# A fused attention and two-MLP kernel: the whole program emitted from one list of operations, with written places for its buffers

## The chip, the cores and the metric

The kernel runs on one core of a Trainium2 chip. TensorE (PE in the profile) multiplies matrices into PSUM, VectorE (DVE), ScalarE (ACT) and GpSimd (POOL) do elementwise work, and SyncE (SP) issues the DMAs. Each engine takes its instructions strictly in the order in which the program emits them. The metric is the time of one execution in device microseconds. Lower is better.

## The reference

```python
q_s = softmax(q over the head dimension); k_s = softmax(k over the sequence)   # float32
kv  = einsum('bhsd,bhse->bhde', k_s, v)
x   = einsum('bhsd,bhde->bhse', q_s, kv)      # 4 batches x 576 tokens -> (2304, 512)
xn  = x / sqrt(mean(x*x) + 1e-6) * rms_g
g   = xn @ w_gate;  val = xn @ w_val          # 512 x 1536, float64 weights
x2  = (silu(g) * val) @ w_out                 # 1536 x 512
out = softplus(x2 @ w2_in) @ w2_out           # 512 x 2048, 2048 x 512
```

Weights arrive in float64 and are converted on the chip. Every product of the MLPs is made from operands split into a high and a low half (`mm3`): three matmuls for each.

## The kernel before, in words

The 2,304 tokens are six blocks `j` of 384. The work has four stages.

1. **Attention and the first third of layer a, from a list.** `ORDER` is a text of 793 entries that a loop emits one by one (L907). It holds the attention, the first 24 weight fetches and conversions, and the first 16 steps of the gate and value products (4 of the 12 slices of `w_gate`, taken plainly) with 15 output steps. Each entry is an operation and its arguments, the last letter being the engine: V for VectorE, P for GpSimd, A for ScalarE. `B.n` emits n filler matmuls of `ident` into a bank that nobody reads (L782).
2. **The rest of those steps** (8 of 24), in a Python loop.
3. **Layer a, Strassen-like.** The other 8 slices are taken in pairs: 12 units (four weight pairs by three pairs of token blocks). A unit has seven products (`SEVEN`) for the gate and seven for the value, each six matmuls of 384 columns (`seven`, L1150), whose sums are copied or added out of PSUM (L1277, L1280), go through silu (L1282, L1288), the product (L1284, L1291) and a split into halves (L1259, L1260). Then come eight output groups of six matmuls (`acc`), which start from a copy of the running sum into PSUM (L1189) and end with a copy back (L1199).
4. **Layer b.** 24 units of seven products `h` (six matmuls each; L1385, L1388, softplus L1322, halves L1324, L1326) and 12 groups of three matmuls of 512 columns (`yacc`, L729 to L731).

Beside these, `convert_some` takes up weight conversions as "jobs" when an estimate of spent engine time (`credit`) allows: absolute value (L253, L249), clamp (L258), three bit operations (L264, L268, L272), sums of pairs (L329 to L332), high half (L310) and low half (L315). Converted weights of layer b and of `w2_out` are written to DRAM from three tiles `ws` (L318, kept<-ws) and read back as `wb` for each unit (L1219). Split token blocks ("quads", L1016 to L1033) go out and come in in the same way (L1037, L1040, L1009, L1012). `advance`, `need`, `more` and `background` decide in the emitting code where these fall between the products; tiles come from rings that turn in the order of use (`w` 16 places, `ws` 3, `raw` 2, `hl` 6, `hb` 5), and PSUM banks are tied to a use (two for each of gate and value, four for `acc`, and so on). All DMAs are issued by SP in one queue, in the order of emission.

In the attention, the values are summed over five chunks of the keys' sequence: four of 128 rows and one of 64 (`k3`, L569).

Of the kernel before, what the change touches and what calls it, by code (L numbers as in the profile page):

```python
# [10 lines left out]
I32 = mybir.dt.int32  # L11
# [14 lines left out]
LQ.0.0 Q0.0.0 QS.0.0.0.V LQ.0.1 LX.0 QE.0.0.0 MX.0 QS.0.0.1.P LK.0.0.1 Q0.0.1 QS.0.1.1.V LK.0.2.2 MK K0.0.0.1.1.R MV  # L26
K0.0.2.2.1.V QE.0.1.1 K0.0.2.2.2.V QE.0.0.1 QS.0.1.0.P LK.0.1.1 K0.0.2.2.3.V LQ.0.2 QE.0.1.0 K0.0.0.1.2.R F.3 LW.0
K0.0.0.1.3.R K0.0.1.1.1.V F.6 K0.0.2.2.4.V F.10 K0.0.1.1.2.V K0.0.0.1.4.R QR.0.0 QI.0.0 QR.0.1 K0.0.1.1.3.V B.29
K1.0.2 KM.0.2 QM.0.0.1.P QI.0.1 CA.3 K0.0.1.1.4.V Q0.0.2 B.9 K1.0.0 K2.0.2 QM.0.1.0.P QS.0.2.0.P CA.10 T.1 CA.6 KM.0.0
K2.0.0 CL.3.V KS.0.2 KS.0.0 QM.0.1.1.P LV.0.4.8 QE.0.2.0 CL.6.V CD.3.0 CD.6.0 CL.10.V QM.0.0.0.P LV.0.0.4 T.2 KE.0.2  # L30
MX.1 CD.3.1 QR.0.2.0 TC.2.A B.4 T.0 CD.10.0 KE.0.0 TC.0.A LQ.1.0 B.1 K3.0.2 F.0 TC.1.A CD.3.2 CA.0 CD.6.1 K3.0.0
CD.10.1 LX.1 QI.0.2.0 Q0.1.0 K4.0.2 K4.0.0 B.2 X0.0.1 CL.0.V LK.1.0.2 LG X0.0.0 CD.6.2 QM.0.2.0.P X0.0.3 CD.10.2
CD.0.0 XG.0.3.A LK.1.2.2 SQ.0.3 CC.6 X0.0.2 F.5 LQ.1.1 QS.1.0.1.P LW.1 QS.1.0.0.P SQ.0.2 K0.1.0.2.1.V CD.0.1
K0.1.0.2.2.V K0.1.2.2.1.V K0.1.0.2.3.V SQ.0.1 LV.1.0.4 K0.1.2.2.2.V QE.1.0.1 K0.1.0.2.4.V K0.1.2.2.3.V CA.5 F.7 CD.0.2
K0.1.2.2.4.V B.3 K1.1.0 SQ.0.0 B.1 K1.1.2 CC.3 CL.5.V XS.0.0.1.P XG.0.2.A XG.0.0.A KM.1.0 LV.1.4.8 KM.1.2 CD.5.0
K2.1.2 K2.1.0 XS.0.2.3.P Q0.1.1 XS.0.0.2.P T.3 X1.0 QS.1.1.1.P QE.1.0.0 KS.1.0 QR.1.0 QS.1.1.0.P XD.0 QI.1.0 T.4 XP.0
CC.0 KE.1.0 QM.1.0.0.P B.3 X2.0 QE.1.1.1 XG.0.1.A KS.1.2 QE.1.1.0 LK.2.0.2 CC.10 K3.1.0 KE.1.2 TC.3.A QR.1.1 CD.5.1
X3.0.2 X3.0.0 CD.5.2 HH.0.0.A QI.1.1 LK.2.2.2 TC.4.A T.5 LX.2 K4.1.0 K3.1.2 QM.1.0.1.P F.1 CS.10.P QM.1.1.0.P CS.3.V
F.4 TC.5.A X3.0.3 X3.0.1 MX.2 K0.2.2.2.1.V HH.0.2.A K4.1.2 X0.1.1 K0.2.2.2.2.V T.6 F.2 X0.1.0 HH.0.3.A X0.1.3
K0.2.0.2.1.R X0.1.2 XG.1.1.A LQ.2.0 QM.1.1.1.P LV.2.4.8 LW.2 HH.0.1.A SQ.1.0 SQ.1.1 SQ.1.2 K0.2.2.2.3.V K0.2.0.2.2.R  # L40
CS.0.P XG.1.2.A T.7 K0.2.2.2.4.V TC.7.A HL.0.0.P K0.2.0.2.3.R SQ.1.3 G.1.0 XS.1.0.1.V K0.2.0.2.4.R T.8 K1.2.2 HL.0.1.P
TC.8.A XS.1.2.3.P TC.6.A CA.1 KM.2.2 XG.1.0.A XG.1.3.A G.1.1 XS.1.0.2.P HL.0.3.P K1.2.0 CA.4 K2.2.2 X0.2.0 HL.0.2.V
G.1.2 CA.7 KM.2.0 KS.2.2 CL.1.V Q0.2.0 KE.2.2 CD.1.0 X1.1 F.9 CL.4.V X0.2.2 K2.2.0 CC.5 G.1.3 XD.1 X0.2.1 CS.6.P
CD.1.1 XP.1 KS.2.0 K3.2.2 X0.2.3 SQ.2.1 LQ.2.1 CS.5.V S.1 CL.7.V SQ.2.0 QS.2.0.1.P CD.1.2 CD.4.0 LV.2.0.4 CA.2
XG.2.0.A G.0.0 X2.1 CL.2.V G.0.1 CC.1 CA.9 G.0.2 Q0.2.1 MX.3 KE.2.0 CD.7.0 CD.4.1 CD.7.1 QS.2.0.0.V CS.1.P CD.4.2
CD.2.0 CD.7.2 XG.2.1.A CL.9.V QE.2.0.1 V.0 QE.2.0.0 G.0.3 QR.2.0 CC.4 S.0 CD.9.0 LV.3.4.8 K3.2.0 X3.1.0 G.2.0 XG.2.3.A
A.0 G.2.1 CS.4.P CD.9.1 V.1 X3.1.1 X3.1.2 CD.2.1 QI.2.0 CC.7 CD.9.2 F.8 QS.2.1.1.P A.1 CC.9 CS.7.P G.2.2 G.2.3 AH.1.A
X3.1.3 LK.3.0.2 QM.2.0.0.P K4.2.0 CD.2.2 CS.9.P V.2 AL.1.P LK.3.2.2 S.2 AH.0.A CA.8 AL.0.V G.3.0 T.9 HH.1.0.A CC.2 A.2
QM.2.0.1.V G.3.1 QS.2.1.0.P SQ.2.3 F.11 QE.2.1.1 K4.2.2 SQ.2.2 QE.2.1.0 V.3 LX.3 XS.2.0.1.V CS.2.P G.3.2 T.10 HH.1.1.A
# [30 lines left out]
def linear_attention_swiglu_softplus_kernel(  # L80
# [1357 lines left out]
```

## Time and profile before

| | us |
|---|---|
| three runs, median (lowest to highest) | 940.3 (937.82 to 942.64) |
| the profiled execution: span from the first to the last instruction | 941.6 |
| TensorE busy in it | 898.6 |
| VectorE busy | 594.6 |
| ScalarE busy | 494.4 |
| GpSimd busy | 174.0 |

The span of the profiled execution lies 1.3 us above the median of the runs and inside their range; the profile lists no time outside its span. "Busy" of TensorE includes the time in which a matmul drains while the next one streams, so it is no measure of how much work is left to save. The first `g` matmul starts at 53.6 us, the first matmul of a gate product of layer a's units at 240.2, the first `h` at 534.3.

### The profile page before, as it was taken

To read this page: it belongs to the slowest core of one execution; us is meant where nothing else is said; L and a number is where in the kernel's file an instruction comes from. 1 tells how busy PE (TensorE), PEld (TensorE's weight loads), DVE (VectorE), ACT (ScalarE), POOL (GpSimd) and SP (SyncE) were. 2 spreads that over 40 slices of the span, in tenths; PEclk is the share of its full clock that TensorE was granted. 3 is DMA by queue.
4 is the path that set the end of the run, shared out by engine and by line. 5 is a ranking of instruction groups with operands and counts; after the bars stand their busy time and mean duration, and the time that the engine had idled before them with its cause. 6 is when DMAs were issued, how large, how long until landed. Compare 5 with 4: busy or idle time off the path is not lost.

```text
span 941.6 us, 13520 instructions
## 1 busy us (share of the span) xinstructions
PE 898.6 (95%) x4840; PEld 837.2 (89%) x4840; DVE 594.6 (63%) x1043; ACT 494.4 (53%) x1013; POOL 174.0 (18%) x162
## 2 busy tenths in 40 slices
PE   7799999999999799999999799999999999999997
PEld 7689999999999799998898798888989898889896
DVE  7999997766776698887778867572632223222222
ACT  3586543424776677776667673443543334333332
POOL 4566513211121111211111122221000000000000
PEclk9999999999999899999999989999999999999999
DMA  9983533442757689687598629889367565286502
GB/s 233 258 204 102 156 101 115 126 130 74 305 214 298 236 327 333 238 344 279 187 351 315 252 76 395 292 301 380 102 223 279 179 191 177 98 334 196 168 13 67
DMA packets 111523, 203.52 MB, mean 216 GB/s; under 512 B 30305, under 2 KB 71265, under 8 KB 111457
## 3 DMA queue, kind: packets, MB, share of 16 engines
q1 hardware_dynamic: 111456, 202.67, 64.2%
q8 instruction: 38, 0.62, 0.3%
q14 instruction: 29, 0.23, 0.1%
HBM read 155.19 MB, written 47.45 MB: 215 GB/s over the span
## 4 chain that ended last, share of the span: by engine, by line
PE 56%; DVE 20%; DMA 9%; ACT 9%; issue 4%; POOL 1%; SPq 1%; DVEq 0%; ACTq 0%; POOLq 0%
PE yacc L730 5%; PE yacc L731 5%; PE yacc L729 5%; PE h L731 5%; PE h L730 5%; PE h L729 5%; DMA kept<-ws 4%; PE acc L729 3%; PE acc L730 3%; PE acc L731 3%; PE g L729 2%; PE v L729 2%; PE g L731 2%; PE g L730 2%; PE v L730 2%
## 5 line engine op out<-in xcount | busy, mean ns | idle before, releaser
L1388 DVE TENSOR_TENSOR p<-h,p 128x384 f32<-128x384 f32 x72 | 40.0, 555 | 139.2 <-PE h L731 132.6
L729 PE MATMUL h<-quad,wb 128*128 128x384 f32 x336 | 113.6, 338 | 5.0 <-DVE p L1388 3.0
L730 PE MATMUL h<-quad,wb 128*128 128x384 f32 x336 | 114.6, 341 | 0.0
L731 PE MATMUL h<-quad,wb 128*128 128x384 f32 x336 | 114.5, 341 | 0.0
L1322 ACT ACTIVATE p<-p 128x384 f32<-128x384 f32 x72 | 37.9, 527 | 111.5 <-DVE p L1388 111.4
L729 PE MATMUL yacc<-wb,hb 128*128 128x512 f32 x210 | 82.0, 390 | 1.4 <-ACT y L1338 1.4
L731 PE MATMUL yacc<-wb,hb 128*128 128x512 f32 x210 | 82.8, 394 | 0.0
L730 PE MATMUL yacc<-wb,hb 128*128 128x512 f32 x210 | 82.8, 394 | 0.0
L1385 ACT COPY p<-h 128x384 f32<-128x384 f32 x72 | 34.4, 480 | 85.6 <-PE h L731 85.0
L729 PEld LDWEIGHTS h<-quad,wb 128*128 128x128 f32 x336 | 63.4, 189 | 14.2 <-DVE p L1388 4.3
L730 PEld LDWEIGHTS h<-quad,wb 128*128 128x128 f32 x336 | 63.2, 188 | 7.1
L729 PE MATMUL v<-quad,w 128*128 128x384 f32 x168 | 57.8, 344 | 9.0 <-DVE p L1280 7.8
L731 PEld LDWEIGHTS h<-quad,wb 128*128 128x128 f32 x336 | 63.4, 189 | 0.0
L729 PE MATMUL g<-quad,w 128*128 128x384 f32 x168 | 57.4, 342 | 2.6 <-ACT p L1277 2.4
L1260 POOL TENSOR_TENSOR hb<-p,hb 128x384 fp32r<-128x384 f32 x26 | 28.9, 1111 | 161.4 <-ACT hb L1259 131.4
L731 PE MATMUL v<-quad,w 128*128 128x384 f32 x168 | 57.0, 339 | 0.0
L730 PE MATMUL v<-quad,w 128*128 128x384 f32 x168 | 56.9, 339 | 0.0
L731 PE MATMUL g<-quad,w 128*128 128x384 f32 x168 | 56.6, 337 | 0.0
L730 PE MATMUL g<-quad,w 128*128 128x384 f32 x168 | 56.4, 336 | 0.0
L729 PE MATMUL acc<-h,w 128*128 128x384 f32 x152 | 51.8, 341 | 3.8 <-ACT acc L1189 3.8
L272 DVE SCALAR_TENSOR_TENSOR bits<-raw,bits 128x512 int32<-128x512 int32 x62 | 51.4, 831 | 1.6
L730 PE MATMUL acc<-h,w 128*128 128x384 f32 x152 | 51.5, 339 | 0.0
(200 smaller groups left out, 2440.5 us busy)
## 6 DMA issues: line engine op xcount, KB each, us to landing
wb<-kept SPq DMA_DIRECT2D x120, 512.0 KB, 6.0
quad<-outside SPq DMA_DIRECT2D x30, 768.0 KB, 7.6
kept<-ws SPq DMA_DIRECT2D x40, 512.0 KB, 4.8
raw<-in_moe_w_out_dram SPq DMA_DIRECT2D x26, 512.0 KB, 4.0
outside<-quad SPq DMA_DIRECT2D x12, 768.0 KB, 3.7
quad<-outside SPq DMA_DIRECT2D x24, 384.0 KB, 6.5
raw<-in_moe_w_in_dram SPq DMA_DIRECT2D x16, 512.0 KB, 4.2
outside<-quad SPq DMA_DIRECT2D x18, 384.0 KB, 3.1
```

What stands on the lines that cost most here:

```text
L272: nc.vector.scalar_tensor_tensor(out=b, in0=words[:, :, 0], scalar=29, in1=b, op0=ALU.logical_shift_right, op1=ALU.bitwise_or)
L729: nc.tensor.matmul(out=ps, lhsT=wh, rhs=xh, start=first, stop=False, skip_group_check=more)
L730: nc.tensor.matmul(out=ps, lhsT=wh, rhs=xl, start=False, stop=False, skip_group_check=more)
L731: nc.tensor.matmul(out=ps, lhsT=wl, rhs=xh, start=False, stop=last, skip_group_check=more)
L1260: nc.gpsimd.tensor_tensor(out=h[:, 1], in0=a, in1=h[:, 0].bitcast(F32), op=ALU.subtract)
L1322: nc.scalar.activation(out=ln, in_=src, func=AF.Softplus)
L1385: nc.scalar.copy(out=t, in_=bk[b])
L1388: nc.vector.tensor_tensor(out=t, in0=bk[b], in1=t, op=ALU.add)
```

## The change

`ORDER` becomes a text of 3,517 entries that emits the whole program, and a second text, `HOMES`, lists for each kind of buffer (`ps`: the eight PSUM banks; `w`, `raw`, `bits`, `ws`, `h`, `hl` and others) the place that each taking of one gets. `convert_some`, `need`, `advance`, `background`, `more` and the loops over units go. The number of places stays (16 `w`, 3 `ws`, 2 `raw`, 3 `bits`, 6 `hl`, 7 `h`). What is computed, and how, stays too, but for the fifth chunk of the keys: its matmuls take 128 rows, of which the upper 64 of the values are set to zero once.

New operations: `M` gate or value product, `C` copy, `D` sum, `SI` silu, `U` product, `BH`/`BL` halves of an activation, `OP`/`OM`/`OC` output group (copy in, matmuls, copy out), `H`, `HC`, `HD`, `SP` the same for layer b, `Y`, `YE`, `YO` its output, `F`, `CA`, `CL`, `CD` fetch and conversion, `PS` sums of pairs, `WH`/`WL`/`KO` halves of a weight and its store, `WB` load of a stored weight, `ZS`, `ZH`, `ZL`, `ZO`, `ZI` sum, halves, store and load of a quad. The entries ahead of the first `G` are 233, ahead of the first `M` 902, ahead of the first `H` 2,232.

Engines change by entry. Ahead of the first `H`, on VectorE and formerly on ScalarE: 19 `BH`, 27 `WH` (22 of 512 columns), 10 `ZH`, 11 `C`, 17 `OC`, 24 `OP`, 7 `CA`. On VectorE and formerly on GpSimd: 33 `BL`. On GpSimd and formerly on VectorE: 30 `WL` (24 of 512 columns), 28 `PS`, 4 `ZL`, 2 `ZS`. Filler matmuls: `B` of 114 in place of 52 (two instructions each); 110 of them stand ahead of the first `G`. VectorE's entries ahead of the first `G` come to 89 instructions. One more load of ScalarE's table (`PL`) and one more clearing of 64 x 512 elements by GpSimd (in `MV`) are added.

```diff
 ORDER = """
-LQ.0.0 Q0.0.0 QS.0.0.0.V LQ.0.1 LX.0 QE.0.0.0 MX.0 QS.0.0.1.P LK.0.0.1 Q0.0.1 QS.0.1.1.V LK.0.2.2 MK K0.0.0.1.1.R MV
...
+LQ.0.0 Q0.0.0 LQ.0.1 QS.0.0.0.P QS.0.0.1.V Q0.0.1 LK.0.1.1 QE.0.0.1 LX.0 MK QE.0.0.0 K0.0.1.1.1.V B.3.7 K0.0.1.1.2.V
...
+M.5.6.g KO.33.2 OM.4.1.2 OC.4.1.2.A CL.37.V BL.5.0.0.V OM.4.0.0 CD.37.0 CD.36.2 D.6.1.g WH.35.1.V SI.5.5 SI.5.6 U.5.5
+OP.4.0.2.A BL.5.1.1.V M.6.2.g WL.35.1.V M.6.3.g WH.36.1.A ZI.5.22.hl OM.4.0.2 ZI.5.21.qe0 KO.34.1 OM.4.0.1 C.6.0.v.A U.5.6
...
+HOMES = """
+ps 01234567012346071326405614265014263751463046727544710251327432574621574301261213741562710625327451366301740610
...
+ws 0120122210012012010201201210120122021021020010212010020102100120120102021022102102
+ln 010110100101010110101001
...
-    def ring(name="w"):
-
-        n = ring_n[0]
-        ring_n[0] += 1
-        assert n < NW or n - NW in ring_free, n
-        w = w_p.tile([P, 2, 512], F32R, tag="w", name=name)
-        return w, n
+    def take(pool, key, shape, dtype=F32):
+
+        key += next(turns[key]) if key in turns else ""
+        at, kind, tile_ = homes.get(key, (pool, None, None))
+        if kind != dtype:
+            tile_ = at.tile(shape, dtype, tag=key, name=key, bufs=1)
+            homes[key] = at, dtype, tile_
+        return tile_
+    def bank():
+        return take(ps_p, "ps", [P, 512])
+    def ring():
+        return take(w_p, "w", [P, 2, 512], F32R)
...
             for r in range(R + 1):
-                p = P if r < R else SX
                 nc.tensor.matmul(
-                    out=ps[:, i, :], lhsT=ke_t[lo][:p, i, r], rhs=v_t[:p, m, r, :], start=(r == 0), stop=(r == R)
+                    out=ps[:, i, :], lhsT=ke_t[lo][:, i, r], rhs=v_t[:, m, r, :], start=(r == 0), stop=(r == R)
                 )
...
         def v_ones(_=None):
             nc.gpsimd.memset(v_t[:, :, :, 2 * D:], 1.0)
+            nc.gpsimd.memset(v_t[SX:, :, R, :2 * D], 0.0)
...
+        def a_copy(u, k, n, e):
+            tag = "ln" if k == 2 else {"g": "s", "v": "a"}[n]
+            t = part[u, k, n] = take(late[0] if k == 2 else fa, tag, [P, T])
+            copy[e](out=t, in_=bk[u, n, SEVEN[k][3]])
+        def load_b(u, name):
+            n = 256 if name == "hx4" else 512
+            w = wb[name, u] = ring()
+            nc.sync.dma_start(out=w[:, :, :n].bitcast(F32), in_=kept[name, u % NPB])
...
-        for t in ORDER.split():
-            t = t.split(".")
-            ops[t[0]](*(int(x) if x.isdigit() else x for x in t[1:]))
-        listed[0] = False
+        for t in ORDER.split():
+            t = t.split(".")
+            ops[t[0]](*(int(x) if x.isdigit() and not (i == 1 and t[0] in texts) else x for i, x in enumerate(t[1:])))
```

## Rows read from the trace of the kernel before

**Rows 1.** The page's first part: busy us (share of the span) and instructions.
```profile
PE 898.6 (95%) x4840; PEld 837.2 (89%) x4840; DVE 594.6 (63%) x1043; ACT 494.4 (53%) x1013; POOL 174.0 (18%) x162
```
**Rows 2.** Busy time by stretch: length, then each engine's busy us (instructions), clock, DMA.
```profile
0.00:53.60 53.60, 42.98 (x275) 37.90 (x276) 46.52 (x99) 26.28 (x46) 30.45 (x36) 0.97 1.08 255
53.60:240.20 186.60, 185.71 (x1099) 178.54 (x1098) 154.23 (x287) 93.80 (x171) 64.11 (x54) 1.00 0.41 116
240.20:534.30 294.10, 278.68 (x1550) 270.21 (x1550) 235.44 (x398) 208.98 (x468) 51.16 (x47) 0.98 0.77 285
534.30:941.60 407.30, 391.27 (x1921) 350.54 (x1919) 158.43 (x262) 165.35 (x331) 28.26 (x26) 0.99 0.60 207
...
186.00:228.00 42.00, 42.00 (x244) 42.00 (x243) 29.32 (x45) 14.53 (x30) 6.54 (x6) 1.00 0.35 115
```
**Rows 3.** Timeline of TensorE in layer b: start us, us.
```profile
849.70 0.39 PE L729 MATMUL yacc<-wb,hb 128*128 128x512 f32 x1
...
850.39 0.33 PE L729 MATMUL h<-quad,wb 128*128 128x384 f32 x1
...
851.46 0.39 PE L729 MATMUL yacc<-wb,hb 128*128 128x512 f32 x1
```
**Rows 4.** Whom TensorE waited for, 240.2 to 534.3: us, times, longest.
```profile
PE v L729 <- DVE p L1280: 7.8, 2, 7.4
PE acc L729 <- ACT acc L1189: 3.1, 3, 1.9
```
**Rows 5.** Timeline around 304 us: start us, us, idle before and its releaser.
```profile
310.27 0.41 ACT L310 CAST ws<-sums 128x256 fp32r<-128x256 f32 x1 [9.50 <-DMA kept<-ws]
...
311.66 0.69 PE L729 MATMUL v<-quad,w 128*128 128x384 f32 x1 [7.39 <-DVE p L1280]
```
**Rows 6.** Chain that ended last: start us, us, what.
```profile
121.06 2.81 PE kvp L569 x20
128.20 0.67 PE rsb L701 x6
```
**Rows 7.** VectorE by line, 240.2 to 534.3: busy, mean ns, idle before.
```profile
L272 DVE SCALAR_TENSOR_TENSOR bits<-raw,bits 128x512 int32<-128x512 int32 x34 | 31.0, 911 | 1.2
L268 DVE SCALAR_TENSOR_TENSOR bits<-raw,bits 128x512 int32<-128x512 int32 x34 | 27.1, 798 | 0.3
L1280 DVE TENSOR_TENSOR p<-g,p 128x384 f32<-128x384 f32 x36 | 19.9, 552 | 1.0 <-PE g L731 0.5 <-ACT p L1277 0.3
L1284 DVE TENSOR_TENSOR p<-p,p 128x384 f32<-128x384 f32 x35 | 19.6, 559 | 4.1 <-ACT p L1282 0.5
L264 DVE TENSOR_SCALAR bits<-bits 128x512 int32<-128x512 int32 x34 | 19.4, 572 | 1.2
...
L315 DVE TENSOR_TENSOR ws<-bits,ws 128x512 fp32r<-128x512 f32 x21 | 14.4, 688 | 12.5 <-ACT ws L310 12.5
L258 DVE TENSOR_SCALAR bits<-bits 128x512 f32<-128x512 f32 x34 | 14.4, 423 | 4.0 <-ACT bits L253 4.0
```
**Rows 8.** VectorE and GpSimd by line, whole span.
```profile
L828 DVE CAST h<-a 128x384 fp32r<-128x384 f32 x9 | 4.4, 485 | 0.1
...
L330 DVE TENSOR_TENSOR bits<-bits 128x256 f32<-128x256 f32 x16 | 6.8, 426 | 0.5
...
L292 POOL TENSOR_TENSOR w<-bits,w 128x512 fp32r<-128x512 f32 x5 | 7.4, 1477 | 3.8 <-ACT w L288 3.8
```
**Rows 9.** DMA issues: count, KB, median us to landing; then a landing in the chain.
```profile
wb<-kept SPq DMA_DIRECT2D x120, 512.0 KB, 6.0
...
kept<-ws SPq DMA_DIRECT2D x40, 512.0 KB, 4.8
...
615.52 10.39 DMA kept<-ws
```
**Rows 10.** Start and end: VectorE's first listed work, TensorE's last matmul.
```profile
5.01 1.22 DVE L594 TENSOR_REDUCE qm<-qh 128x16 f32<-128x1024 f32 x1 [2.67 <-DMA qh<-in_q_dram]
...
935.30 0.39 PE L731 MATMUL yacc<-wb,hb 128*128 128x512 f32 x1
```

More of the change, by code (lines that the diff above doesn't have):

```diff
@@ L225, in fetch @@
         else:
[L226 removed]
+            raw = take(raw_p, "raw", [P, 2 * 512], I32)
         r64 = raw.bitcast(I64)
@@ L432, in need, with take_up @@
-    def need(*keys):
-        i = 0
-        while not all(k in ready for k in keys):
-            now[0] += 1
-            convert_some(True)
-            i += 1
-            assert i < 100, (keys, jobs, ring_n)
-    at = ExitStack()
-    kv_p = at.enter_context(tc.tile_pool(name="kv", bufs=1))
-    q_p = at.enter_context(tc.tile_pool(name="q", bufs=2))
-    sm_p = at.enter_context(tc.tile_pool(name="sm", bufs=2))
+        return name, p, o
+    def take_up(n):
+        b = bits[n] = bits_tile(n)
+        nc.sync.dma_start(out=b, in_=spilled[n])
@@ new lines, in make_l, with keep_w @@
+    def make_l(n, x, e):
+        key, src, off, w = part_of(n, x)
+        t = wt[key]
+        c = slice(off, off + w)
+        engine[e].tensor_tensor(out=t[:, 1, c], in0=src, in1=t[:, 0, c].bitcast(F32), op=ALU.subtract)
+    def keep_w(n, x):
+        key, _, _, w = part_of(n, x)
+        d = kept[key] = dram.tile([P, 2, w], F32, tag=f"{key[0]}{key[1]}", name="kept", bufs=1)
+        nc.sync.dma_start(out=d, in_=wt.pop(key)[:, :, :w].bitcast(F32))
+    attention = ExitStack()
+    kv_p = attention.enter_context(tc.tile_pool(name="kv", bufs=1))
@@ L496, in load_q @@
         else:
-            t = q_p.tile([P, H, 2, D], F32, tag="qh", name="qh")
+            t = take(q_p, "qh", [P, H, 2, D])
             nc.sync.dma_start(
@@ L778, in x2_out, with busy @@
                 nc.scalar.copy(out=x2t[j][:, m], in_=ps)
-        idle = []
-        def busy(n):
-            if not idle:
-                idle.append(bank("busy", 7, 8))
+        def busy(_, n):
+            ps = bank()
             for _ in range(n):
-                nc.tensor.matmul(out=idle[0][:, :P], lhsT=ident, rhs=ident[:, :BW], start=True, stop=True)
+                nc.tensor.matmul(out=ps[:, :P], lhsT=ident, rhs=ident, start=True, stop=True)
         run = {}
@@ L812, in s_step @@
         def s_step(i):
-            s = run["s", i] = fa.tile([P, T], F32, tag="s", name="s")
+            s = run["s", i] = take(fa, "s", [P, T])
             nc.scalar.activation(out=s, in_=run.pop(("g", i))[:, :T], func=AF.Silu)
@@ L971, in release, with start_late @@
-        def release(r, name):
-            place = place_of.pop((r, name))
-            quad.pop((r, name))
-            if place[0] == "hl":
-                hl_rel.add((r, name))
-            free.append((*place[:-1], now[0]))
+            "TU": take_up,
+            "PS": pair_sum,
+            "WH": make_h,
+            "WL": make_l,
+            "KO": keep_w,
+        }
+        def start_late():
+            attention.close()
+            late.append(ctx.enter_context(tc.tile_pool(name="late", bufs=1)))
@@ L1150, in seven, with quad_in @@
+        def quad_in(r, name, at):
+            d = outside[RUNS[r][1], name]
+            w = quad_tile(r, name, at)
+            if w is not None:
+                nc.sync.dma_start(out=w.bitcast(F32), in_=d)
+            else:
+                for m in range(2):
+                    nc.sync.dma_start(out=quad[r, name][m].bitcast(F32), in_=d[:, m])
         def seven(ps, w, off, x, first):
```

1177 lines of the change are left out of this document (516 added, 661 removed).

## The prediction, on record before the changed kernel ran

> **What bounds the kernel now.** I read the page's first part, then the busy times by stretch, the timeline where TensorE is densest, and the waits. The page gives TensorE 95% of the span [rows 1], but a busy matmul may be one that drains while the next streams, so I counted matmuls by their start-to-start time. Where nothing disturbs them, 244 matmuls of 384 columns take 42.00 us, 0.172 each [rows 2]; in layer b three `yacc` take 0.69 us (0.23 each) and six `h` 1.07 (0.178 each) [rows 3]. Against these rates each stretch of [rows 2] shows what it loses:
>
> - 0 to 53.6: the wait for the first `g`. The list before has about 23 us of TensorE work other than fillers ahead of it, so some 31 us are lost; VectorE is busy 46.52 us of the 48.6 that follow its first reduction [rows 2, 10]. VectorE sets this stretch.
> - 53.6 to 240.2, also from a list: TensorE stands idle 0.9 us, although VectorE is busy 83% of the time.
> - 240.2 to 534.3, layer a from the emitting rules: 1550 x 0.172 = 266.6, so 27.5 of 294.1 us are lost. The reader is to see that TensorE waits for evacuations, 7.8 and 3.1 us [rows 4], and that the largest is an accident of order: a cast into a `ws` tile waited 9.50 us for the store of the tile's former content, ScalarE's layer work stood behind it, and TensorE waited 7.39 us for a bank [rows 5]. The rest is short waits and matmuls at half clock behind the gaps.
> - 534.3 to the end: 1008 `h` and 864 `yacc` at [rows 3] are 179.4 + 198.7 = 378.1, the remaining 49 matmuls 8.4, the tail behind the last matmul 6.3 [rows 10]: 14.5 of 407.3 us are lost.
>
> So TensorE bounds the kernel from 53.6 us on, with some 42 us of waits in the two stages that no list orders, and VectorE bounds the first 53.6.
>
> **The change part by part.** *Matmuls.* All products stay. The fifth chunk: 20 matmuls of a `kvp` group take 2.81 us, 0.1405 each, while six full-height ones of 128 columns take 0.67, 0.112 each [rows 6]. At the full-height rate a group is 2.23, so 0.58 less. Two of the eight groups lie in the first stretch, which VectorE sets; six give 3.5 us. I take -3; bounds 0 (a gap covers it) and -4.6 (all eight).
>
> *Fillers.* 62 more, 124 instructions at about 0.112 = 13.9 us. They run where TensorE waits in the start (31 us), so I take 0; without that cover they would cost up to 13.9, and with the 49 ahead of the first transposes just reaching the time at which VectorE is done, I keep +3 as the bound.
>
> *Start.* Priced by the mean durations of the trace, VectorE's instructions listed ahead of the first `G` come to 57 us against 52 in the old list. They overlap a little, and not each is needed. I take +3; bounds -4 and +6.
>
> *Layer a.* Waits like that of [rows 5] go if the list keeps distance. The model for what a list does is the stretch 53.6 to 240.2, 0.5% idle at 83% VectorE. But layer a will be denser on VectorE, so I do not carry 0.5% over. Work on VectorE ahead of the first `H`, from the counts of the change: on to it 19 `BH` at 0.485 [rows 8] = 9.2; 27 `WH`, no row, between 0.485 and 0.688 for a full one, taken 0.6 (quarter of the small ones less) = 15; 10 `ZH`, no row, between 0.7 and 0.97 (two casts of 384), taken 0.85 = 8.5; 52 copies into or out of PSUM at 0.55, the nearest row being `L1280`'s 0.552 = 28.6; 7 `CA` at 0.688 = 4.8; 33 `BL` at 0.559 = 18.4 [rows 7]. Sum 84.5. Off it: 24 `WL` at 0.688 and 6 at about 0.43 = 19.1; 28 `PS` at 0.426 = 11.9; 6 `ZL` and `ZS` at about 0.95 (estimate: 768 columns at `L1284`'s rate less its fixed part) = 5.7. Sum 36.7. Net +47.8.
>
> GpSimd gains too: off it 33 `BL` at 51.16/47 = 1.09 [rows 2] = 36; on to it 24 `WL` at 1.48 [rows 8] and 6 at half of that = 40; 28 `PS` at 0.75 too = 21; 6 quads at two times 1.09 = 13; less a few in the attention. About +36 on the 145.7 us of the first three stretches.
>
> That matters because GpSimd delays VectorE. In layer a `L272`, `L268` and `L264` take 911, 798 and 572 ns where their like take 688, 688 and 423, while `L1280`, which reads PSUM, keeps 552 [rows 7]: 34 x (0.223 + 0.110 + 0.149) = 16.4 us lost on 51.16 us of GpSimd, 0.32 per us. At that price +36 us cost VectorE 11.5.
>
> The Trainium skill, page "SBUF — State Buffer", section "Who interferes with whom", says that a VectorE instruction with two SBUF inputs and a GpSimd instruction that reads SBUF exclude each other, the second one blocking until the first has finished. By it the added 36 us would cost up to 36 and not 11.5; the unharmed `L1280` agrees with it, and the 0.32 says that most of GpSimd's time met a VectorE that was idle or read PSUM. At that full price VectorE's need below would be 525 in place of 500.5, 8 us past the first `H` that I take, and the forecast 924.
>
> VectorE's need up to the first `H` is then 436.2 (its busy time in three stretches, [rows 2]) + 47.8 + 11.5 = 495.5, from 5.0 on: 500.5. ScalarE loses the 82 us or so that VectorE and others take over and stays under 75%.
>
> TensorE's side: 534.3 + 3 - 3 less what layer a gives back. I take a loss of 10 in place of 27.5, between 4 (idle as in the listed stretch, plus clock) and 27.5 (no gain): 17.5. First `H` at 516.8, with VectorE's 500.5 close behind: 97% busy. That closeness is why I keep 10.
>
> *Layer b.* VectorE needs about 40% there. What is lost is waits for `wb` loads, late stores and evacuations; 14.5 becomes 7, between 3 and 14.5: -7.5. The added load of ScalarE's table (1.3 us) and the clearing by GpSimd lie beside TensorE's work; uncovered they are 1.3 and 0.6.
>
> *SP's queue.* The number and size of transfers stay. The list takes a `w` place by name, so a load waits for that place's last matmul and everything behind it in SP's queue waits too. Counted along the list in TensorE time, of 144 `wb` loads 12 have at most 8.6 us between the moment at which SP can issue them and their first matmul, the least 4.1; the row says 6.0 to land [rows 9]. Of 48 reuses of a `ws` tile behind a store 17 have at most 8.4 us, the least 2.1; a store lands in 4.8, in a bad case in 10.39 [rows 9]. At median landings the shortfall is about 7 us on each of the two, most of it on ScalarE and VectorE and taken up by banks in hand: inside the 10 and the 7.
>
> Sum on the profiled execution: 941.6 + 3 - 3 - 17.5 - 7.5 = 916.6. The median of the runs lies 1.3 lower: 915.3, forecast 916.
>
> **The rivals.** *Better (905).* The list is as good in layers a and b as in the attention: losses 4 and 4, start unchanged: 941.6 - 3 - 23.5 - 10.5 = 904.6, as a median 903. For it speaks the listed stretch; against it that VectorE had 17% to spare there.
>
> *Late transfers (937).* Stores and loads land at 10 us rather than 5 to 6. The shortfalls counted as above are then about 77 us on `ws` and 49 on `wb`; if a sixth of it reaches TensorE, +21. For it: layer a's DMA share is 0.77 [rows 2], and one such wait cost 7.39 [rows 5]. Against: one stall gives the next transfer its time.
>
> *VectorE becomes the bound (958), slower.* The place is layer a. VectorE idles 20% there now, and that idle time is where GpSimd's instructions do no harm. When it is 97% busy, each us of GpSimd costs more than 0.32. All of GpSimd's 182 us ahead of the first `H` count. The first `H` must come at 546 for the kernel to be 0.5% slower (546 + 407.3 - 7.5 = 945.8, less 1.3), so VectorE must need 45.5 us more than 495.5, a price of 0.32 + 45.5/182 = 0.57 per us of GpSimd. At 0.65 it is 60 more: first `H` at 560.5, 960.3 in the profile, 959 as a median. The 0.32 of layer a, at 80% busy, speaks against a doubling. The rule of the Trainium skill named above would allow it.
>
> **How the numbers follow.** Forecast 0.52, better 0.19, late transfers 0.16, VectorE the bound 0.13. A change of 0.5%, 4.7 us, is about what the runs can tell from none (they spread over 4.8), so faster is under 935.6 and slower over 945.0. The forecast and the better case are faster, of late transfers 0.4, of VectorE's case 0.05: 0.78. The same: half of late transfers and a fifth of VectorE's case: 0.11. Slower: 0.11. Predicted 916; the range 898 to 943 leaves out the best of the better case and most of VectorE's.
>
> **What would show it.** First `g` within 50 to 60 us; `kvp` groups of 2.2 to 2.4 us; first `h` near 517 with VectorE over 90% busy from 230 to 517; GpSimd at about 285 us in all; `L272` and its like slower than 911 ns where VectorE is dense; in layer b no wait of TensorE over 2 us. The prediction fails if TensorE's longest waits are for VectorE's sums in layer a (VectorE's case), if ScalarE waits for kept<-ws or `h` for `wb` by many us (late transfers), or if the start moves by 10 us.

## The result, and the profile after

The kernel after takes 917.28 us in the median of four runs (914.94 to 919.39), the kernel before 941.47 in the median of four beside them: a ratio of 0.9746, 95% interval 0.9707 to 0.9784. The forecast was 916. The profiled execution of after has a span of 913.2 us and a time of 914.94, so 1.7 us of it lie outside the span, which I had taken as nothing; and it is the fastest of the four. Where one profile is set against another below, differences under some 4 us say little.

The page's first part, after (busy us, share of the span, instructions):

```profile
PE 894.1 (98%) x4964; PEld 842.5 (92%) x4964; DVE 623.9 (68%) x1155; ACT 408.3 (45%) x820; POOL 285.1 (31%) x250
```

Against [rows 1] ScalarE is busy 86 us less, VectorE 29 more and GpSimd 111 more. The busy times by stretch (length, PE, PEld, DVE, ACT, POOL, clock, DMA, GB/s), cut at the first `G`, the first `M` and the first `H`:

```profile
0.00:58.10 58.10, 51.78 (x392) 48.78 (x393) 49.92 (x106) 28.47 (x48) 24.38 (x32) 0.97 0.95 242
58.10:225.77 167.67, 166.31 (x1005) 160.61 (x1004) 140.98 (x263) 84.53 (x155) 70.62 (x59) 1.00 0.39 110
225.77:511.70 285.93, 282.72 (x1622) 280.50 (x1622) 261.26 (x487) 162.49 (x357) 87.63 (x75) 1.00 0.85 306
511.70:913.20 401.50, 393.32 (x1951) 352.57 (x1950) 171.74 (x303) 132.83 (x261) 102.43 (x86) 1.00 0.62 208
```

The cuts don't fall at the same work as in [rows 2]: the list starts layer a and layer b while matmuls of the stage ahead are still to come. 102 matmuls fewer lie ahead of the first `M`, and some 30 fewer ahead of the first `H`. At 0.172 us each the changes at equal work are: start +4.5; listed stretch 167.67 + 17.5 against 186.6, so -1.4; layer a 285.93 less 72 x 0.172 = 273.5 against 294.1, so -20.6; layer b 401.5 less 30 x 0.172 = 396.3 against 407.3, so -11.0. Together that is -28.5, the difference of the two spans (28.4) but for rounding. Counted as in the prediction, layer a lost 27.5 us and now loses 285.93 - 1622 x 0.172 = 6.9.

What TensorE waited for in layer a after (whom, us, times, longest):

```profile
PE ps L838 <- ACT ps L1148: 2.5, 3, 1.5
PE ps L838 <- DVE s L1119: 0.3, 1, 0.3
PE ps L838 <- ACT x L1157: 0.3, 1, 0.3
```

The wait of 7.4 us [rows 4] is gone. The waits that the profiles list for TensorE in layer a fall from 14.9 us in all to 3.1. The granted clock counts too: before had two stretches at half (the lower of its two levels, 1.2 of 2.4 GHz), the first 1.5 us after a wait of 1.94 us had ended, the second in the middle of the wait of 7.39.

```profile
263.31:266.72 3.41, 3.41 (x13) 3.41 (x12) 2.55 (x4) 3.41 (x7) 0.00 (x0) 0.50 0.78 317
307.69:314.51 6.82, 2.85 (x9) 2.85 (x10) 3.43 (x7) 3.66 (x8) 1.01 (x1) 0.50 0.68 266
```

TensorE worked 6.3 us in them, so they cost about 3 us (an estimate: half of that time); after has no such stretch in layer a. What is left of the 20.6 stands in no list of waits.

In layer b before waited so:

```profile
PE acc L729 <- ACT acc L1189: 3.8, 2, 2.3
PE h L729 <- DVE p L1388: 3.0, 3, 1.6
PE h L729 <- ACT p L1385: 2.0, 1, 2.0
```

And after:

```profile
PE ps L838 <- DMA wf<-kept: 2.3, 1, 2.3
PE ps L838 <- ACT a L1187: 1.1, 1, 1.1
```

These two are new, and both are looked at below. The tail behind the last matmul is shorter too: that matmul starts at 908.83 of 913.2, before at 935.30 of 941.6 [rows 10].

### The profile page after: what moved, and what is told of

Read it like the earlier page. It is cut to its first block, busy times and chain, and to the rows that moved or that the text cites. A ratio compares the mean times of both kernels' runs of the same rounds, so it can differ in the third digit from the quotient of the medians.

```text
span 913.2 us, 13708 instructions
## 1 busy us (share of the span) xinstructions
PE 894.1 (98%) x4964; PEld 842.5 (92%) x4964; DVE 623.9 (68%) x1155; ACT 408.3 (45%) x820; POOL 285.1 (31%) x250
## 4 chain that ended last, share of the span: by engine, by line
PE 70%; DMA 11%; DVE 10%; ACT 3%; issue 2%; SPq 2%; POOL 1%; ACTq 0%; DVEq 0%; POOLq 0%
PE ps L838 23%; PE ps L839 23%; PE ps L840 22%; DMA kept<-ws 5%; DMA k_t<-in_k_dram 2%; DMA raw<-in_moe_w_in_dram 2%; DVE bits L469 1%; DVE bits L465 1%; PE ps L684 1%; DVE km_t L634 1%; SPq L594 1%; DMA xy<-outside 1%; DMA raw<-in_moe_w_val_dram 1%; PE ps L885 1%; DMA w<-kept 1%
## 5 line engine op out<-in xcount | busy, mean ns | idle before, releaser
L838 PE MATMUL ps<-hl,w 128*128 128x384 f32 x280 | 98.2, 351 | 0.2 <-DVE xy L815 0.2
L839 PE MATMUL ps<-hl,w 128*128 128x384 f32 x280 | 93.8, 335 | 0.3 <-DVE hl L835 0.3
L840 PE MATMUL ps<-hl,w 128*128 128x384 f32 x280 | 93.8, 335 | 0.0
L1179 DVE TENSOR_TENSOR s<-ps,s 128x384 f32<-128x384 f32 x48 | 26.6, 556 | 88.0 <-PE ps L840 80.2
L838 PE MATMUL ps<-xy,w 128*128 128x384 f32 x226 | 76.3, 338 | 1.0 <-DVE s L1119 0.3
L1144 POOL TENSOR_TENSOR h<-s,h 128x384 fp32r<-128x384 f32 x29 | 30.7, 1064 | 148.1 <-DVE h L1140 81.5
L840 PE MATMUL ps<-xy,w 128*128 128x384 f32 x226 | 75.9, 336 | 0.0
L839 PE MATMUL ps<-xy,w 128*128 128x384 f32 x226 | 75.8, 335 | 0.0
L1144 POOL TENSOR_TENSOR h<-a,h 128x384 fp32r<-128x384 f32 x29 | 32.1, 1111 | 128.3 <-ACT h L1140 65.8
L840 PE MATMUL ps<-w,h 128*128 128x512 f32 x180 | 71.2, 395 | 0.0
L839 PE MATMUL ps<-w,h 128*128 128x512 f32 x180 | 70.9, 394 | 0.0
L838 PE MATMUL ps<-w,h 128*128 128x512 f32 x180 | 70.1, 390 | 0.2 <-DMA w<-kept 0.2
L838 PE MATMUL ps<-h,w 128*128 128x384 f32 x192 | 64.7, 337 | 2.7 <-ACT ps L1148 2.3
L840 PE MATMUL ps<-h,w 128*128 128x384 f32 x192 | 64.2, 334 | 0.0
L839 PE MATMUL ps<-h,w 128*128 128x384 f32 x192 | 64.2, 334 | 0.0
L839 PEld LDWEIGHTS ps<-hl,w 128*128 128x128 f32 x280 | 52.6, 188 | 2.1 <-DVE hl L835 0.5
L838 PEld LDWEIGHTS ps<-hl,w 128*128 128x128 f32 x280 | 52.6, 188 | 2.1 <-DVE xy L815 0.6
L1187 ACT ACTIVATE s<-s 128x384 f32<-128x384 f32 x48 | 24.8, 524 | 64.6 <-DVE s L1179 64.5
L840 PEld LDWEIGHTS ps<-hl,w 128*128 128x128 f32 x280 | 52.6, 188 | 0.0
L469 DVE SCALAR_TENSOR_TENSOR bits<-raw,bits 128x512 int32<-128x512 int32 x62 | 49.8, 808 | 0.9
L465 DVE SCALAR_TENSOR_TENSOR bits<-raw,bits 128x512 int32<-128x512 int32 x62 | 48.6, 787 | 0.7
L450 ACT ACTIVATE bits<-raw 128x512 f32<-128x512 f32 x49 | 32.7, 672 | 31.5 <-DMA raw<-in_moe_w_in_dram 6.5
```

The lines of the kernel that those rows point to most:

```text
L450: nc.scalar.activation(out=b.bitcast(F32), in_=hi, func=AF.Abs)
L465: nc.vector.scalar_tensor_tensor(out=b, in0=words[:, :, 1], scalar=-0x40000000, in1=b, op0=ALU.bitwise_and, op1=ALU.bitwise_or)
L469: nc.vector.scalar_tensor_tensor(out=b, in0=words[:, :, 0], scalar=29, in1=b, op0=ALU.logical_shift_right, op1=ALU.bitwise_or)
L838: nc.tensor.matmul(out=ps, lhsT=wh, rhs=xh, start=first, stop=False, skip_group_check=more)
L839: nc.tensor.matmul(out=ps, lhsT=wh, rhs=xl, start=False, stop=False, skip_group_check=more)
L840: nc.tensor.matmul(out=ps, lhsT=wl, rhs=xh, start=False, stop=last, skip_group_check=more)
```

## Experiments

Two theories stood against each other for layer a. *Order*: the list keeps distance between a write and its use, so no engine's queue stands behind a late store. *Engines*: ScalarE was overloaded, and handing 108 of its operations in layer a to VectorE made the gain. Beside them the smaller terms and the rivals of the prediction were tried. "After" below is its second timing, e5, unless said otherwise.

| run | median us | ratio to before, 95% interval |
|---|---|---|
| e1 after, fifth chunk 64 rows | 921.52 | 0.9804 (0.9783 to 0.9825) |
| e2 before, fifth chunk 128 rows | 940.17 | 1.0000 (0.9983 to 1.0018) |
| e3 after, no fillers | 917.56 | 0.9759 (0.9739 to 0.9779) |
| e4 after, former engines in layer a | 926.85 | 0.9855 (0.9834 to 0.9876) |
| e5 after again | 917.48 | 0.9766 (0.9739 to 0.9793) |
| e6 after, VectorE and GpSimd exchanged back | 925.11 | 0.9833 (0.9814 to 0.9852) |
| e7 after, ScalarE's work given back | 923.98 | 0.9823 (0.9806 to 0.9841) |
| e8 after, late load covered | 913.92 | 0.9717 (0.9699 to 0.9735) |
| e9 before, engines shared as in the list | 973.23 | 1.0350 (1.0329 to 1.0372) |
| e10 after, fewer table loads | 916.12 | 0.9752 (0.9729 to 0.9774) |
| e11 after, improved | 909.51 | 0.9677 (0.9649 to 0.9705) |
| e12 after, more GpSimd work | 929.91 | 0.9880 (0.9858 to 0.9901) |

**The yardstick (e5).** 

> The kernel after, unchanged, as the yardstick for the runs beside it and for how far one profiled execution of it lies from another (its first profile, at 913.2, lies under all its timed runs). Expected 917, a ratio of 0.975, with the first g at 58 to 61 us and the first h at 512 to 517.

917.48 us. In its profile the first `G` comes at 58.4, the first `H` at 510.3; the runs that leave the start and layer a untouched put them at 57.6 to 60.2 and 510 to 517. So two profiles of one list differ by a few us in either stage. The runs of the table stand beside three timings of before, whose medians are 939.58 (e1 to e4), 941.34 (e5 to e8) and 940.34 (e9 to e12). By the ratios, which allow for that, e4 lies 8.4 us above after and e12 10.7, where the medians say 9.4 and 12.4.

**The fifth chunk, undone in after (e1) and alone in before (e2).**

```diff
 e1, kernel after:
+                p = P if r < R else SX
-                    out=ps[:, i, :], lhsT=ke_t[lo][:, i, r], rhs=v_t[:, m, r, :], start=(r == 0), stop=(r == R)
+                    out=ps[:, i, :], lhsT=ke_t[lo][:p, i, r], rhs=v_t[:p, m, r, :], start=(r == 0), stop=(r == R)
-            nc.gpsimd.memset(v_t[SX:, :, R, :2 * D], 0.0)
 e2, kernel before: the opposite of these lines
```

> The kernel after, with the keys' fifth chunk through 64 rows again and without the extra clearing; all else as after. If the fifth chunk's rows reach the end, it gives back the term that the prediction took for it, about 3 us (0 to 4.6): about 920, 0.978 of the time before, with groups of 20 kvp matmuls back from some 2.3 to some 2.8 us. If the gaps of the list cover it, the time stays at 917 and only the groups lengthen.

> The kernel before, with this one part of the change: the fifth chunk through 128 rows and the one clearing by GpSimd. By the prediction's term 3 us less, 938, a ratio of 0.997; if it is covered, 1.000. Either way it is no more than an eighth of the change's 24 us, so the rest must be in the list.

e1 took 4 us more than after, with intervals that overlap slightly; e2 took the same as before, to within 1.7 us. The first two groups of 20 matmuls in the chain of after (start us, us):

```profile
73.24 2.23 PE ps L684 x20
...
83.04 2.41 PE ps L684 x20
```

and the first of six such in the chain of e1:

```profile
49.74 2.82 PE ps L685 x20
```

The price of a group is as predicted (2.8 to 2.2 or 2.4). Whether it reaches the end depends on the kernel around it. In e1 six of the eight groups lie on the chain, two of them ahead of the first `g`; in after three do. In e2's listed stretch the four groups gave 2.2 us by start-to-start time, and 1.0 us was left at its end (185.6 against 186.6 us). The timing does not show even that.

**No fillers (e3).** `B.k.n` became `B.k.0`.

> The kernel after without its 114 filler matmuls (each B entry still takes its bank, and emits none). Theory of the prediction: they run where TensorE waits for VectorE, so the first g stays at 58 us and the total within 2 us of after, 915 to 919. Rival one, the fillers delay the start (the first g came 4.5 us later than before): it moves forward by 3 to 5, total 913. Rival two, they keep the granted clock up: without them the clock of the first 60 us falls below 0.97, the matmuls that end the start take longer, and the total rises by 3 to 6, 920 to 923.

917.56 us, no change: the prediction's zero holds. The first stretch of e3:

```profile
0.00:60.49 60.49, 32.49 (x173) 28.46 (x174) 50.50 (x106) 28.21 (x48) 24.69 (x32) 0.89 0.96 240
```

Against after TensorE is busy 19.3 us less and VectorE the same 50. The clock did fall, from 0.97 to 0.89, as rival two said, but the total did not rise. VectorE, busy for 50 of 60 us, sets the start with or without fillers.

**The engines of layer a as before (e4), and each half of that (e6, e7).** Letters between the first `M` and the first `H` only; order and places stay.

```diff
 e4 = both; e6 = the first line; e7 = the second
-33 BL.V, 26 WL.P, 25 PS.P, 3 ZL.P, 1 ZS.P, 1 CL.P
+33 BL.P, 26 WL.V, 25 PS.V, 3 ZL.V, 1 ZS.V, 1 CL.V
-24 OP.V, 23 WH.V, 19 BH.V, 17 OC.V, 11 C.V, 8 ZH.V, 6 CA.V
+24 OP.A, 23 WH.A, 19 BH.A, 17 OC.A, 11 C.A, 8 ZH.A, 6 CA.A
```

> The kernel after, with the engine letters between the first layer-a product and the first h set as the rules before had them: 108 operations from VectorE back to ScalarE, 33 low halves from VectorE back to GpSimd, 56 operations from GpSimd back to VectorE. Order and places stay. Worked out from the durations after, ScalarE rises from 162 to about 222 us in that stretch of 286, VectorE falls from 261 to about 205, GpSimd from 88 to about 57. Theory order: layer a's gain comes from the distances in the list, so the first h stays within 8 us of 512 and the total is 917 to 925. Rival engines: ScalarE's relief made it, so most of layer a's 20 us come back: 932 to 940, with TensorE waiting for ScalarE's copies.

> The kernel after with one half of the former engines in layer a: 33 low halves from VectorE back to GpSimd, and 56 operations (26 low halves of weights, 25 pair sums, 5 others) from GpSimd back to VectorE. By durations after, VectorE gains about 12 us net in a stretch of 286 where it is busy 261, GpSimd loses about 30. Theory, the exchange with GpSimd buys VectorE's room: VectorE is at 95% and more, it waits less for nothing, and the total rises by 3 to 8, 920 to 925. Rival, ScalarE's relief is what counted in the run with all former engines: no change here, 917.

> The kernel after with the other half: 108 operations of layer a from VectorE back to ScalarE, which rises to about 222 of 286 us, while VectorE falls to some 195. Theory, ScalarE's relief made the 9 us that the run with all former engines gave back: 924 to 928, with TensorE waiting for ScalarE's copies into PSUM. Rival, the GpSimd exchange made them: 917 to 919, since VectorE now has a third of its time free.

The same stretch, first `M` to first `H`, in e4:

```profile
224.84:522.33 297.49, 288.28 (x1622) 281.73 (x1621) 229.82 (x400) 208.99 (x468) 59.35 (x48) 0.99 0.81 294
```

and TensorE's longest waits in it:

```profile
PE ps L837 <- ACT ps L1147: 7.3, 8, 3.3
PE ps L837 <- DVE s L1118: 0.8, 2, 0.6
```

In e6:

```profile
225.81:523.35 297.54, 287.36 (x1621) 281.76 (x1621) 269.99 (x511) 162.52 (x357) 57.46 (x49) 0.99 0.81 294
```

```profile
PE ps L837 <- DVE s L1118: 3.1, 3, 1.9
PE ps L837 <- DVE a L1118: 2.4, 3, 1.5
```

And in e7:

```profile
227.07:522.44 295.37, 286.43 (x1622) 280.24 (x1622) 218.94 (x376) 209.22 (x468) 84.79 (x75) 1.00 0.82 296
```

```profile
PE ps L837 <- ACT ps L1147: 5.7, 8, 1.9
```

All three lose 16 to 19 us in layer a (length less 0.172 a matmul) where after and e5 lose 7 and other runs of the same list up to 11. e4's 9.4 us over after is more than the theory of order allowed and less than that of engines. The halves cost 7.6 and 6.5, close to what the theory of each had (920 to 925 and 924 to 928 in all), and do not add. In e6 TensorE waits for VectorE's sums; in e4 and e7, where ScalarE is busy 70%, it waits for ScalarE's copies into banks (L1147, the list's `OP`), which now stand in a longer queue. Each half alone is enough to unbalance a list that was ordered for the other shares. No list ordered for the former shares was tried, so what order alone can give is at least what e4 shows.

**The engines alone, under the old rules (e9).**

```diff
+    def cast(key, of, out, in_):
+        (nc.vector.tensor_copy if shift(key, of) else nc.scalar.copy)(out=out, in_=in_)
-                nc.scalar.copy(out=ps, in_=x2t[2 * jp + o][:, m])
+                cast('op', {1, 5, 9, 13, 17}, ps, x2t[2 * jp + o][:, m])
...
```

(`shift` counts and answers yes for the named ones of 20, in layer a; the other casts and low halves in the same way.)

> The kernel before, its emitting rules kept, with the engines of layer a shared out in about the proportions of the list: of the copies into acc one in four, of those out of it one in five, of the copies of sums one in seven, of the casts of activations two in five, of the casts of weights and of whole quads one in two on VectorE instead of ScalarE; three in four low halves of activations on VectorE instead of GpSimd; half of the low halves of weights and half of the pair sums on GpSimd instead of VectorE. Theory engines: the share alone gives the 8 to 10 us in layer a that the list loses without it, 931 to 934. Theory order: the share pays only where the list gives each operation its time; under the rules VectorE's queue now holds what ScalarE's held, and the time is 938 to 946.

33 us slower than before: both theories had it too fast. Its layer a:

```profile
238.09:561.99 323.90, 286.38 (x1550) 271.67 (x1549) 282.76 (x488) 159.81 (x359) 74.62 (x66) 0.97 0.70 259
```

and its timeline around 313 us (start us, us, what, idle before and its releaser):

```profile
313.84 0.29 DVE L306 CAST ws<-sums 128x256 fp32r<-128x256 f32 x1 [10.41 <-DMA kept<-ws]
...
315.12 0.55 DVE L1292 TENSOR_TENSOR p<-v,p 128x384 f32<-128x384 f32 x1
...
315.25 0.69 PE L741 MATMUL g<-quad,w 128*128 128x384 f32 x1 [9.46 <-DVE p L1292]
```

This is the accident of [rows 5] again: the cast into a `ws` tile waits 10.41 us for the store of its former content. Now it waits on VectorE, so the sums stand behind it, and TensorE loses 9.46 us where it had lost 7.39. This wait comes with the rules' order; the engine decides who stands behind it. But it makes only 2 of the 30 us by which the stretch grew. Most of them are many waits for VectorE's sums:

```profile
PE g L741 <- DVE p L1292: 14.3, 5, 9.5
PE v L741 <- DVE p L1292: 6.0, 4, 2.3
```

TensorE's listed waits come to 37 us here, 15 in before. VectorE is busy 282.8 us with 488 instructions, where after's list needs 261.3 for 487. ScalarE was relieved to 160 us, as far as in after, and that alone bought nothing. One thing was left as it was: the rules' estimate of spent time (`credit`) still charges conversions as though the former engines did them. How much of the 33 us comes from that was not tried.

**More work on GpSimd (e12),** for the slower rival.

```diff
+            for _ in range(n):                     # GP.4 behind each of 26 WL.P in layer a
+                nc.gpsimd.tensor_tensor(out=ident, in0=ident, in1=ident, op=ALU.mult)
```

> The kernel after with 104 more products of 128 columns on GpSimd in layer a, four behind each of 26 low halves of weights; they read and write only the identity matrix, which nobody uses by then, so the output stays. At about 0.5 us each (from 0.83 for 256 columns and 1.47 for 512) 53 us more on GpSimd in a stretch where it is busy 88 of 286. If a us of GpSimd costs VectorE 0.3, as after shows on the whole, VectorE rises by 16 us from 91% to 97% and the total by 2 to 6, 919 to 923. If it costs 0.8, as where the two overlap on SBUF, VectorE needs 303 us in 286 and the total is 930 to 940, the slower rival of the prediction. If what matters is only where they meet, less than 0.3 and no change.

The added group, and then the stretch:

```profile
L949 POOL TENSOR_TENSOR ident<-ident 128x128 f32<-128x128 f32 x104 | 56.5, 543 | 6.1
```

```profile
224.69:525.73 301.04, 288.98 (x1622) 281.40 (x1622) 275.14 (x486) 163.19 (x358) 144.74 (x179) 0.99 0.80 291
```

56.5 us more on GpSimd made VectorE busy 13.9 us longer, 0.25 per us, the low price. Yet the stretch grew by 15.1 us and the kernel by 12.4. TensorE now waits for VectorE there:

```profile
PE ps L838 <- DVE ps L1153: 2.9, 2, 2.6
PE ps L838 <- DVE s L1124: 2.5, 5, 1.0
```

VectorE's share is 91.4% in after and 91.4% here, and in none of ten profiles read by this stretch is it higher. So in this layer and this order VectorE seems to be as full as it gets at 91%, and what is added to it comes out at the end nearly one for one. That 91% is a limit is inferred, not shown: in after 10 of its 24.7 us of idle time end with a sum from TensorE, which the fixed order can't fill, and in e12 VectorE also waits longer for GpSimd's results, 5.6 us where after has 2.3.

**The late load (e8).** After's SP queue, and the matmul that waited:

```profile
642.04 0.42 SPq L557 DMA_DIRECT2D kept<-ws  x1
648.95 0.32 SPq L1164 DMA_DIRECT2D wf<-kept  x1
...
652.92 0.47 PE L838 MATMUL ps<-wf,h 128*128 128x512 f32 x1 [2.29 <-DMA wf<-kept]
```

The store is `KO.66.1`, the last half of `w2_out`; the load is `WB.7.y0`, of the same data. The place of the load was free at about 646, but SP issued the load only when the store had landed, at 648.90, after 6.4 us in which it issued nothing; the load landed at 652.8. Everything behind it in SP's queue waited too. And TensorE lost more than the wait. From 1.4 us after it the granted clock is at half:

```profile
654.30:657.70 3.40, 3.40 (x11) 2.71 (x10) 0.96 (x2) 0.00 (x0) 0.60 (x1) 0.50 0.05 17
```

That is some 1.7 us more (an estimate: half of the stretch), so the late load cost about 4.

```diff
-Y.7.1.0.0 Y.7.1.1.1 ... H.8.4 H.8.3
+Y.7.1.1.1 H.8.4 H.8.3 Y.7.1.0.0
```

> The kernel after with three entries of layer b put ahead of the first matmul that needs the last stored weight of w2_out: one output group and two h products, 2.8 us of TensorE. In the profile of after TensorE waits 2.3 us there for a load that could be issued only when the store of the same data had landed. If that wait is simply late data, it goes and the total falls by 2 to 2.5, 915; if the queue behind it only shifts, another wait of that size appears within 30 us and the total stays.

The wait is gone from the profile, none of its size followed, and layer b has no stretch at half clock. The time fell by 3.6 us, more than the 2 to 2.5 expected for the wait alone; the 4 us with the clock agree better. By the profiles, first `H` to end is 398.1 us, and 400.0 to 403.1 in the eight profiles that leave layer b as in after.

**Table loads (e10).** ScalarE's table loads from 511.7 to 630 us in after:

```profile
L1187 ACT ACT_TABLE_LOAD x5 | 6.4, 1283 | 0.1
L450 ACT ACT_TABLE_LOAD x4 | 5.1, 1283 | 0.1
L1234 ACT ACT_TABLE_LOAD x1 | 1.3, 1283 | 0.0
```

Before has one in that place. The old rules moved the absolute value to VectorE once softplus had begun; the list leaves four on ScalarE (L450) between softplus (L1187), and each costs a load there and one back. At one place it reached TensorE:

```profile
624.45 0.68 ACT L450 ACTIVATE bits<-raw 128x512 f32<-128x512 f32 x1
...
625.15 1.28 ACT L1187 ACT_TABLE_LOAD   x1
...
626.99 0.44 PE L838 MATMUL ps<-qe,w 128*128 128x384 f32 x1 [1.13 <-ACT a L1187]
```

The Trainium skill, page "ScalarE: Activation LUTs", section "Table sets: the hidden batching unit", says that functions come in sets, that a change of set costs a load of about 2.7 us, and that abs is in every set. The first agrees with the trace. From the end of the `Abs` to the start of the next Softplus 1.31 us passed here, so for the price the measurement decides. An `Abs` behind a Softplus did load; between 151 and 518 us, where `Abs` alternates with silu, there is no load. Whether Softplus's set lacks abs, or the load was put there without need, no run here shows.

```diff
-CA.59.A ... CA.61.A ... CA.66.A ... PL ... CA.67.A
+CA.59.V ... CA.61.V ... CA.66.V ... CA.67.V
```

> The kernel after with four absolute values of layer b (CA.59, 61, 66, 67) on VectorE instead of ScalarE and without the entry PL. The profile of after shows ten loads of ScalarE's table behind the first h, 1.28 us each, where before has one: the list puts Abs between Softplus. Expected: one load is left there, about 11 us less on ScalarE, TensorE's wait of 1.1 us at the last pair of loads goes, total 1 us less, 916.5; VectorE takes 2.7 us more, covered, since it is busy under half of that stage. If ScalarE's time beside TensorE were worth more, 912 to 914.

One load is left and the wait is gone, but 916.12 us can't be told from after. The profile has 397.8 us from the first `H` to the end, 2 us under the lowest of the eight that leave layer b as it was. So the 11 us of ScalarE beside TensorE were worth little: the one wait that they caused, and perhaps a little more.

**An improved version (e11).** e8 and e10 together, and in layer a two conversions moved:

```diff
-CA.32.A ZI.3.t4.hl F.33 OP.3.0.2.A ... OP.3.0.3.A CL.32.V
+ZI.3.t4.hl F.33 OP.3.0.2.A ... OP.3.0.3.A CA.32.A CL.32.V
-CA.52.A ... OC.7.0.3.A ... OP.8.0.0.A OC.7.0.0.A ... CL.52.V M.10.1.v OP.8.1.1.A
+OC.7.0.3.A ... OP.8.0.0.A OC.7.0.0.A ... M.10.1.v OP.8.1.1.A CA.52.A CL.52.V
```

The reason is this in the timeline of after: ScalarE waits for a fetched weight with the copy for the next output group (L1148) behind it, and TensorE with it.

```profile
468.42 0.67 ACT L450 ACTIVATE bits<-raw 128x512 f32<-128x512 f32 x1 [1.10 <-DMA raw<-in_moe_w_in_dram]
...
469.89 0.44 PE L838 MATMUL ps<-h,w 128*128 128x384 f32 x1 [1.47 <-ACT ps L1148]
```

> The kernel after with the edits that the traces point to: the three entries of the run on the late load, the four absolute values on VectorE without PL, and in layer a two ScalarE conversions that wait for a fetch (CA.32, CA.52) put behind the copies into banks that stood behind them. Waits of TensorE shown in after: 2.3, 1.1, 0.9 and 1.5 us. Expected sum 5 to 6 less than after, 911.5 to 912.5, a ratio of 0.969.

909.51 us, 8.0 less than after (expected 5 to 6), intervals apart. Its longest wait from the first `M` on is

```profile
PE ps L837 <- ACT ps L1147: 1.1, 1, 1.1
```

and first `H` to end takes 395.6 us, 5 to 6 less than in after's two profiles. Layer a's stretch is 286.9, as in after, so the moved conversions aren't shown to have given anything.

## Why the prediction was right, and where not

**The sum.** The forecast of 916 for 917.28 is closer than its parts, and partly by luck. The sum for the span was 916.6, and the profile has 913.2: all four parts together gave 3.4 us more than predicted. From the span to the median I took 1.3 us off; in after it is 4.1 us on, 1.7 outside the span and the rest because the fastest run was profiled. The two misses largely cancel.

**Start.** Predicted +3, measured +4.5; other runs of the same list put it between +3 and +7. VectorE's bound holds: it is busy 49.9 us of it, with fillers or without (e3).

**Fillers.** Zero, as predicted.

**Fifth chunk.** The price of a group was right, the count not: two of eight groups were taken to lie in the first stretch, and four do (16 of the 32 64-row matmuls in either stretch). So at most the 2.2 us that e2's four groups gave, not 3.5, stood to be gained behind it. The runs give nothing under the old rules (e2) and about 4, with an uncertainty of as much, under the list (e1). What makes that difference is open.

**Layer a.** Predicted -17.5, measured -20.6; the loss went from 27.5 to 6.9 (predicted 10). The sum was right and the mechanism half of it. I credited the list's distances with all of it, and treated the change of engines as a load that VectorE had just to bear. e4 says that this order with the old engines leaves a loss of 18.5, so order alone is worth at least 9; e9 says that the new shares under the former rules, as they stood, cost 33. The other 8 to 12 came only with both together.

**VectorE's need.** This step failed in its sum, and it seems in its limit too. The need ahead of the first `H` was put at 495.5, 97% of the time to then. Measured are 49.92 + 140.98 + 261.26 = 452.2. One cause is mine: I added durations to busy times. Instructions of one engine overlap a little, and the windows count such time once; the groups of that stretch sum to 503 where the windows show 452, and in before to 470 where they show 436. So the overlap grew by 17 us, which the sum left out. The other is the price of GpSimd: 11.5 us more were expected on VectorE, and what VectorE's durations exceed the tenth percentile of their like by rose from 22 to 28 us in layer a, so by 6, although GpSimd has 36 us more there. These two make some 23 of the 43 us that were predicted too much; the other 20 are not accounted for. The limit was set near 100%, and e12 speaks for 91%. If so, two errors of opposite sign met in a right answer: the predicted need against that limit, 495.5/0.91 = 544.5, would have come near VectorE's case (546).

**What GpSimd costs.** "`L272` and its like slower than 911 ns" was wrong. Layer a of after, the same operations (busy us, mean ns, idle before):

```profile
L469 DVE SCALAR_TENSOR_TENSOR bits<-raw,bits 128x512 int32<-128x512 int32 x32 | 23.5, 741 | 0.6
L465 DVE SCALAR_TENSOR_TENSOR bits<-raw,bits 128x512 int32<-128x512 int32 x32 | 23.3, 734 | 0.4
...
L1119 DVE TENSOR_TENSOR s<-ps,s 128x384 f32<-128x384 f32 x24 | 13.2, 551 | 2.8 <-PE ps L840 2.7
```

They fell from 911 and 798 [rows 7], with VectorE denser and 71% more GpSimd time beside it. What happens is seen in a few lines of after's timeline:

```profile
295.64 0.56 DVE L1119 TENSOR_TENSOR s<-ps,s 128x384 f32<-128x384 f32 x1
296.05 1.28 POOL L552 TENSOR_TENSOR wb<-ws,wb 128x512 fp32r<-128x512 f32 x1
296.12 1.77 DVE L465 SCALAR_TENSOR_TENSOR bits<-raw,bits 128x512 int32<-128x512 int32 x1
...
297.80 0.68 DVE L469 SCALAR_TENSOR_TENSOR bits<-raw,bits 128x512 int32<-128x512 int32 x1
```

The sum that reads PSUM keeps its 0.56 beside GpSimd; the bit operation that begins under GpSimd's 1.28 us takes 1.77 in place of 0.68, 1.09 more. Counted in the traces of layer a, 23 of 34 `L272` met no GpSimd before and took 692 ns, and 27 of 32 `L469` after, 687. Of the 72 `L1119`, 39 ran beside GpSimd and stayed at 550; in before 9 of the 71 `L1280` did. The list has GpSimd work more often beside VectorE's reads of PSUM, and so it pays less per us. The Trainium skill, page "SBUF — State Buffer", section "Who interferes with whom", has it that a VectorE instruction with two SBUF inputs and a GpSimd instruction that reads SBUF shut each other out, and that a VectorE instruction with at most one SBUF input, outside the 2-port modes, does not contend. Both agree with these rows: the bit operation reads two tiles in SBUF, the sum one. The average of 0.3 per us was a matter of meeting, as the prediction said.

**GpSimd's total.** Predicted about 285 us, measured 285.1.

**Layer b.** Predicted -7.5, measured -11.0. TensorE's listed waits fell from 10.2 us to 4.1, as forecast; the shorter tail (4.4 us from the start of the last matmul against 6.3) was not in the sum. "No wait over 2 us" was wrong by one, the load of e8. It is close to the place that the rival of late transfers named (`h` for `wb`; here an output product waits for it), with another cause: not a slow landing of the load (3.8 us, less than the 6.0 of [rows 9]) but a store and a load of the same data in sequence. The count along the list took a load as free to go when its place was free, and missed that.

**Table.** "One more load of ScalarE's table" was nine more (20 against 11 in all), and one wait of TensorE followed from them, at the last pair.

**The rivals.** *Better* did not come by itself; e11 comes within 7 us of its 903 by removing waits one by one. *Late transfers* cost one wait. *VectorE the bound* was closer than its price says: by what VectorE's durations exceed the tenth percentile the price fell, from 22/51.16 = 0.43 to 28/87.63 = 0.32, and what e12 added cost 0.25; but the stage had little room left, and e6 and e12 show what a little more would have done, 925 and 930.

## What to carry to other kernels

The share of work between engines and the order of each engine's queue have to be chosen together: the list with the former shares gave back 9 of its 24 us, and the new shares under the former rules cost 33. Ask how full an engine can get before it sets the pace, and test it by adding work; here it came to no more than 91% as the windows count it. In an ordered list look for three things by name: an operation that waits for a transfer with an evacuation behind it, a load of what has just been stored, and activation functions that alternate.

## What was not expected of the hardware

A 64-row matmul instruction of 129 columns in the fifth chunk took 0.208 us from start to start, where most of 128 rows took 0.11 in the same groups of before. The 128-row instruction just ahead of the pair of 64-row ones (0.202) and the one just behind it (0.214) were slow too. With 128 rows throughout, as in after, all take 0.11, so that padding with zeros nearly halves the time. Why fewer rows take longer no run here shows. And an Abs that follows a Softplus came with a load of ScalarE's table, 1.28 us each way.
